# A transformer block in fp32: k, v and q by Strassen block products

## The chip, the cores and the metric

The kernel runs on one core of one Trainium2 chip. Its engines are TensorE (PE in the profile, its weight loads PEld), VectorE (DVE), ScalarE (ACT), GpSimd (POOL) and SyncE (SP), whose queue issues the DMAs here. The metric is the device time of one execution in microseconds; before the change it is 506.88 us, the median of three runs.

## The reference

From x (2048 tokens of 512 features, fp32) a layer norm without parameters gives xn. Two branches start there, and the output joins them.

```
qkv = xn @ wqkv                       # q, k, v: 32 heads of 16
pq, pk = q, k @ w_phi, head by head
phi = [softmax(p), softmax(-p)]       # over 16, so 32 per head
kv = phi_k^T v;  z = sum of phi_k over the tokens
s  = (phi_q kv / (phi_q z + 1e-6)) @ wo
g  = silu(mish(xn @ w1 + b1) @ w2)    # 512 -> 1792 -> 512
out = x + s * g
```

## The kernel before

**Exact products.** Each fp32 factor is split into a high part of type fp32r and a low part, the rest: ScalarE copies (the rounding), VectorE or GpSimd subtracts (`split`). A product of two such factors is three matmuls, low·high, high·low and high·high, accumulated in a bank of PSUM (`mm3`, or the inner loop of `product`).

**Tiles.** The tokens lie in 16 tiles of 128. Part `N` (`norm`) loads a tile of x, normalizes it, transposes it on TensorE into bank `pt`, splits it into tile `xT`, copies it raw into `xr`, and stores both to DRAM (`scr`, `raw`). Parts `K`, `V` and `Q` (`k_proj`, `v_proj`, `q_proj`) take one tile each: 4 chunks of 128 features by 3 matmuls of 128x512. The weights of k and q have w_phi folded in on TensorE (`fold`); `q_proj` loads its tile back from `scr` (tile `xq`). The softmax of k and q reads the bank and a copy of it (`kp`, `qp`), subtracts the maximum or minimum, and goes through exp on ScalarE, a sum and a reciprocal. Part `A` (`kv_acc`) adds phi_k^T v into bank `kvp`, `z` closes it, `D` (`den`) forms the denominators and transposes phi_q on VectorE into `ph`, `Ua`/`Ub` multiply with kv (`pn`), `O` (`att_out`) with wo (`pw`).

**FFN1** (parts `Fa` to `Fd`, 14 pieces n = 7 blocks of w1 by 2 halves of the tokens) uses Strassen's form already: seven products instead of eight for a 2x2 block product. Weight sums come from `P` (`prep1`) and `M` (reloaded), the x blocks and their sums from `L` (`load_g`): b11, b21, b22 from `scr`, four differences t1 to t4 from the raw tiles, then split. Accumulating sums in PSUM and additions on VectorE (`plus`) form the four output blocks. **FFN2** (`G`, closed by `E`, `final`) uses seven products too, from `R` (`prep2`), of 128x256 each; its first two of seven blocks are direct.

**Order.** Every operation is recorded first. `ORDER` lists the parts; TensorE runs their matmuls in exactly that order. For the other engines and the DMA queue a list scheduler (`simulate`) orders the operations: each has a latest time, taken from the matmul it feeds, and is started when its engine is free and its buffers fit. `copy` may go to ScalarE or VectorE, `either` to VectorE or GpSimd. `locks` names the operations that take a port shared by these two; the planned clock `port` makes the later one wait. `PEN` is added to the latest time of an operation when VectorE could leave it to another engine. Buffers: 38 slots of 4 KB per partition, 11 of 2 KB (`s2`), 2 of 16 KB (`tq`), 8 PSUM banks.

All calls are issued by line 351, so groups are told apart by tile names.

Of the kernel before, what the change touches and what calls it, by code (L numbers as in the profile page):

```python
# [28 lines left out]
PEN, HOLD, MARGIN = 2000, 300, 1000  # L29
# [8 lines left out]
wq0 wk0 N4 N2 N1 N8 wk1 wv1 wv0 N0 K1 V0 K0 K4 N5 K2 wq1 V2 N3 K5 V3 V1 K3 N9 A0 V4 V5 K8 b1 P2 N7 N6 K9 A1 A2 P3 V7  # L38
K7 K6 N12 P0 V6 N10 N11 L0 V8 K11 V9 Fa0 Fa3 K10 A3 A4 V11 V12 V10 Fb3 Fb0 Fc3 Fc0 K12 N14 Fd3 N13 P6 N15 Fd0 K14 A5
K15 V13 K13 P1 Fa1 Fa6 P4 V15 V14 Q3 Fb6 Fc6 Q2 Fb1 A7 A6 Fc1 Q0 Fd1 P5 z Q7 M2 Fa5 Fd6 D3 Fa4 Q4 Q1 Fb5 Fa2 Fc5 Fb2  # L40
Fb4 Q9 D2 Fc2 D7 Q12 Fd2 Fc4 Fd5 M4 Q5 D4 Q15 L1 Fa9 Fb9 Fd4 Fa11 Fb11 D1 Q6 Fc11 D6 M1 M6 Fc9 Fd11 Fd9 D0 Fa8 D12
Fa13 Fb13 Fc13 M0 Q10 Fb8 Fc8 Fd13 wo1 D9 D15 Fa7 D5 Fb7 Q8 Fd8 M3 Fc7 M5 Q11 Fd7 Fa10 Fa12 D8 D10 Fb12 Fb10 Fc10 Ua0
Fc12 Fd10 Fd12 Ub0 wo0 Q14 Q13 O6 D11 O1 D14 R4 O2 O7 O5 O3 D13 Ua1 O4 Ub1 O0 O11 O15 O12 O8 O13 R0 O9 R5 R1 R6 O14 G0
R2 G1 G2 R3 G3 O10 G4 G5 G6 G7 G8 G9 G10 G11 G12 G13 G14 G15 G16 G17 G18 G19 E0 G20 G21 G22 G23 G24 G25 E1 E2 G26 G27
G28 G29 G30 G31 G32 E3 G33 G34 G35 G36 G37 G38 G39 E4 G40 G41 G42 G43 G44 G45 G46 G47 E5 G48 E6 G49 G50 G51 E7
# [4 lines left out]
class Op:  # L50
    __slots__ = ("impl", "reads", "writes", "at", "idx", "succ", "ndep", "late", "new", "ready", "start", "eng", "sets", "slack", "open", "soon", "pos", "deps", "lock", "part", "half", "code")


class Program:


    def __init__(self, nc):
        self.eng = {"PE": nc.tensor, "V": nc.vector, "G": nc.gpsimd, "A": nc.scalar, "Q": nc.sync}
        self.ops, self.tag, self.cap, self.pe = [], {}, {}, []
        self.group, self.slack, self.part, self.half = None, SLACK, None, False  # L60

# [34 lines left out]

    def add(self, impl, reads, writes, sets=()):
        o = Op()
        o.code = sum(self.records(*c) for c in impl["PE"][1]) if "PE" in impl else 0
        o.impl, o.reads, o.writes, o.idx, o.sets, o.slack = impl, reads, writes, len(self.ops), sets, self.slack  # L100
        o.pos, o.part, o.half = len(self.pe), self.part, self.half
        self.half = False
        o.lock = {e for e, (_, calls) in impl.items() if any(locks(e, m, a) for m, a, k in calls)}
        if "PE" in impl:
            self.pe.append(o)
        self.ops.append(o)

    def call(self, e, m, a, k):
        aps = [v for v in list(a) + list(k.values()) if isinstance(v, bass.AP)]
        w = {aps[0].tensor.name} - {"out"}  # L110
        r = {v.tensor.name for v in aps[1:]}
# [36 lines left out]
    def links(self):  # L148
# [22 lines left out]
        for o in ops:  # L171
            o.new = []
            for n in o.reads | o.writes:
                if n in self.tag:
                    self.uses[n] = self.uses.get(n, 0) + 1
                    if n not in self.first:
                        self.first[n] = o
                        o.new.append(n)

    def simulate(self, at):  # L180
# [22 lines left out]
        dma = port = 0  # L203
# [83 lines left out]
        while left:  # L287
# [8 lines left out]
            for kind, i in todo:  # L296
# [6 lines left out]
                elif kind == 1:  # L303
                    o = ops[i]
                    left -= 1
                    for n in o.reads | o.writes:
# [15 lines left out]
            for e in ("A", "V", "G", "Q"):  # L322
                if busy[e] > now or e == "Q" and (dma > now + BACK or lanes[-LANES:][0:1] > [now] and len(lanes) >= LANES):
                    continue
                skip = []
                while ready[e]:
                    late, i = heapq.heappop(ready[e])
                    o = ops[i]
                    if o.start is not None:
                        continue  # L330
# [9 lines left out]
                for s in skip:  # L340
                    heapq.heappush(ready[e], s)
        return sorted(ops, key=lambda o: (o.start, o.idx))
# [34 lines left out]
def block_kernel(ctx: ExitStack, tc: tile.TileContext, x, wqkT, wv, phi, wo, w1, b1, w2, out):  # L377
# [98 lines left out]
    def fold(wT, name, i):  # L476
        hi = slot([P, 2, D], f"{name}h{i}", F32R)
        lo = slot([P, 2, D], f"{name}l{i}", F32R)
        for j in range(2):
            ps = bank([P, D], f"{name}f{i}{j}")  # L480
            with one():
                for g in range(KC):
                    PE.matmul(ps[:, g * P:(g + 1) * P], wT[2 * i + j][:, g, :], phit[:, g, :], start=True, stop=True)
            split(ps, hi[:, j, :], lo[:, j, :])
        return [(hi[:, j, :], lo[:, j, :]) for j in range(2)]
# [7 lines left out]
    def load_pair(src, name, i):  # L493
        t = slot([P, 2, D], f"{name}r{i}")
        Q.dma_start(t, src[2 * i * P:2 * (i + 1) * P, :].rearrange("(c p) k -> p c k", p=P))
        hi, lo = split_raw(t, f"{name}{i}")
# [3 lines left out]
    scr = [dram.tile([P, 2, KC, 4, P], F32, name=f"scr{g}") for g in range(NG)]  # L500
    raw = [dram.tile([P, KC, 4, P], F32, name=f"raw{g}") for g in range(NG)]
    xT = {}
# [6 lines left out]
    def norm(t):  # L509
# [8 lines left out]
        w = slot([P, 2, KC, P], f"xT{t}", F32R)  # L518
# [9 lines left out]
        split(pt, w[:, 0], w[:, 1])  # L528
        xT[t] = w
        xr = s2(f"xr{t}")  # L530
        copy(xr, pt.rearrange("p k n -> p (k n)"))
        Q.dma_start(raw[t // 4][:, :, t % 4, :], xr.rearrange("p (k n) -> p k n", k=KC))
        Q.dma_start(scr[t // 4][:, :, :, t % 4, :], f32(w))

    def proj(t, w, name):
        ps = bank([P, D], f"{name}{t}")
        for i in range(0, KC, 2):
            with one():
                for k in (i, i + 1):
                    mm3(ps, (xT[t][:, 0, k, :], xT[t][:, 1, k, :]), w[k], k == 0, k == KC - 1)  # L540
        return ps


    def softmax(ps, name, r):
        p = s2(f"{name}p")
        copy(p, ps)
# [22 lines left out]

    kvp = bank([P, 4, 64], "kvp")  # L570
    zacc = slot([P, 2 * D], "zacc")
    ek, eq, rq, phT, oT = {}, {}, {}, {}, {}

    def k_proj(t):
        r = sm([P, 2 * H], f"k{t}r")
        e = softmax(proj(t, w["k"], "k"), f"k{t}", r)
# [3 lines left out]
    def q_proj(t):  # L580
        xT[t] = slot([P, 2, KC, P], f"xq{t}", F32R)
        Q.dma_start(f32(xT[t]), scr[t // 4][:, :, :, t % 4, :])
        rq[t] = alloc("rq", [P, 2 * H], f"q{t}r")
        eq[t] = softmax(proj(t, w["q"], "q"), f"q{t}", rq[t])

    def v_proj(t):
        copy(vb[t % 4], proj(t, w["v"], "v"))
# [79 lines left out]
    w1_, w2_, fx, ys = {}, {}, {}, {}  # L667
# [45 lines left out]
    def load_g(q):  # L713

        def pair(k, g):
            ts = [slot([P, 2, 4 * P], f"f{'hl'[u]}{k}{g}", F32R) for u in range(2)]
            for u, t in enumerate(ts):
                Q.dma_start(f32(t.rearrange("p k n -> p (k n)")), scr[g][:, u, 2 * k:2 * k + 2].rearrange("p k t n -> p (k t n)"))
            return ts

        def whole(k, g):
            t = slot([P, 2, 4 * P], f"fr{k}{g}")
            Q.dma_start(t.rearrange("p k n -> p (k n)"), raw[g][:, 2 * k:2 * k + 2].rearrange("p k t n -> p (k t n)"))
            return t

        def sub(x, y, name):
            t = slot([P, 2, 4 * P], f"{name}{q}")
            either(t, x, y, op=ALU.subtract)
            return t

        g, h = 2 * q, 2 * q + 1
        b11, b21, b22 = pair(0, g), pair(1, g), pair(1, h)
        r11, r12, r22 = whole(0, g), whole(0, h), whole(1, h)
        t1 = sub(r12, r11, "t1")
        s1 = split_raw(t1, f"t1{q}")
        t2 = sub(r22, t1, "t2")
        s2_ = split_raw(t2, f"t2{q}")
        t3 = sub(r22, r12, "t3")
        s3 = split_raw(t3, f"t3{q}")
        t4 = sub(whole(1, g), t2, "t4")  # L740
        s4 = split_raw(t4, f"t4{q}")
        fx[q] = [b11, b21, b22, s1, s2_, s3, s4]
# [26 lines left out]
    def plus(t, ps):  # L769
        V.tensor_tensor(t, t, ps, op=ALU.add)  # L770

# [9 lines left out]
    def ffn1b(n):  # L781
        x, y = part[n][0], bank([P, D], f"fy{n}")
        product(x, n, 4, 4, False)
        part[n] += [y, held(x, f"hb{n}", 2 * (n % NB))]
        product(y, n, 3, 3, True)

    def ffn1c(n):
        x, y = part[n][:2]
        product(x, n, 5, 5, False)
        h = held(x, f"hc{n}", 2 * (n % NB) + 1)  # L790
        plus(h, y)
        put(n, h, 1, 1)

    def ffn1d(n):
        x, y, h = part.pop(n)
        product(x, n, 2, 6, False)
        put(n, held(x, f"hd{n}", 2 * (n % NB) + 1), 0, 1)
        product(y, n, 6, 2, False)
        plus(h, y)
        put(n, h, 1, 0)  # L800
# [53 lines left out]

    def final(T):
        y = lambda n: ys[T][HOME[T == NQ - 1][n][0]][:, HOME[T == NQ - 1][n][1], :]
        plus_ = lambda o, a, b: V.tensor_tensor(o, a, b, op=ALU.add)
        if T < NQ - 1:
# [13 lines left out]
            for i in range(2):  # L872
                t = 2 * T + 1 - i
# [6 lines left out]
            return  # L880
        c, u2, u3, u4 = (slot([P, D], f"yc{i}")[:, 0:2 * P] for i in range(4))
# [6 lines left out]
        for t, h, base, n in ((2 * T, 1, u5, 8), (2 * T, 0, u3, 4), (2 * T + 1, 1, u4, 3), (2 * T + 1, 0, c, 2)):  # L888
# [14 lines left out]
    w = {n: [None] * KC for n in "kqvo"}  # L903

    def weights_k(i):
        w["k"][2 * i:2 * i + 2] = fold(wkT, "wk", i)

    def weights_v(i):
        w["v"][2 * i:2 * i + 2] = load_pair(wv, "wv", i)

    def weights_q(i):
        wqT[2 * i:2 * i + 2] = load_wT(0, "wq", i)
        w["q"][2 * i:2 * i + 2] = fold(wqT, "wq", i)
# [7 lines left out]
    def sums():  # L921
# [16 lines left out]
        for i in range(4):  # L938
# [6 lines left out]
             "wk": weights_k, "wv": weights_v, "wq": weights_q, "wo": weights_o, "N": norm, "K": k_proj, "V": v_proj, "A": kv_acc, "Q": q_proj, "D": den, "Ua": num_a, "Ub": num_b,  # L945
# [39 lines left out]
```

## Time and profile before

| | |
|---|---|
| runs | 506.66, 506.88, 507.48 us |
| span of the profiled execution, first to last instruction | 505.5 us (no time of its own is listed beside it; the median is 1.4 us above) |
| mean granted TensorE clock | 0.999 |
| moved by DMA | 120.35 MB, mean 238 GB/s |
| instructions | 9803 |

Busy times are sums over an engine's instructions. A matmul's duration includes its way through the array, which the next one overlaps, so pace is read from start to start. A row names the output tile, then its inputs, with numbers left out; "idle before" is the engine's idle time just ahead of that group, and what ended it.

### The profile page before, as it was taken

Reading aid. Unit: us, or ns where it says so; the run is one execution under the profiler, and the core shown is the slowest. Engines: PE = TensorE matmul, PEld = TensorE weight load, DVE = VectorE, ACT = ScalarE, POOL = GpSimd, SP = SyncE. Lnnn points to the kernel's source line nnn. Section 1 sums busy time; section 2 is a strip of 40 time slices with the busy share of each in tenths; the row PEclk is TensorE's granted clock in tenths of the full one; section 3 lists DMA queues with packets and bytes.
Section 4 is the critical chain, followed back from the end, with each engine's and each line's share of the span. In section 5 each row is a group of like instructions: output and inputs, shape, how many; then the busy total and the mean of one; then the engine's idle time right before and its main releaser. Section 6 shows DMA issues by size and latency. Waiting matters only on the chain.

```text
span 505.5 us, 9803 instructions
## 1 busy us (share of the span) xinstructions
PE 496.5 (98%) x3594; PEld 426.6 (84%) x3594; DVE 434.1 (86%) x651; ACT 279.4 (55%) x412; POOL 378.1 (75%) x271
## 2 busy tenths in 40 slices
PE   8999999999999999999999999899999999999996
PEld 7888888888887888888888777678899999999996
DVE  5999999978879787999997899998768679978764
ACT  4865765465545332553233356587685775958611
POOL 2489999288786565686579558999789779789860
PEclk9999999999999999999999999999999999999999
DMA  8799898829987999889979762825463467665441
GB/s 307 227 336 302 294 346 278 269 105 316 294 295 251 332 319 326 291 233 318 337 240 345 255 229 78 294 89 188 146 209 118 147 204 241 236 199 171 147 146 63
DMA packets 96191, 120.35 MB, mean 238 GB/s; under 512 B 7568, under 2 KB 65040, under 8 KB 96144
## 3 DMA queue, kind: packets, MB, share of 16 engines
q1 hardware_dynamic: 96000, 119.70, 71.2%
q8 instruction: 28, 0.46, 0.4%
q14 instruction: 19, 0.16, 0.1%
q10 hardware_dynamic: 144, 0.03, 0.0%
HBM read 71.08 MB, written 48.63 MB: 237 GB/s over the span
## 4 chain that ended last, share of the span: by engine, by line
PE 89%; DVE 9%; ACT 1%; issue 0%; DMA 0%; DVEq 0%; ACTq 0%
PE y L351 28%; PE fx L351 15%; PE v L351 8%; PE fy L351 8%; PE q L351 8%; PE k L351 7%; PE pw L351 5%; PE fz L351 4%; PE pn L351 2%; PE kvp L351 2%; PE wake L351 1%; PE pt L351 1%; DVE ph L351 1%; DVE tz L351 1%; DVE ol L351 1%; DVE q13e L351 1%
## 5 line engine op out<-in xcount | busy, mean ns | idle before, releaser
L351 POOL TENSOR_TENSOR al<-r,ah 128x896 fp32r<-128x896 f32 (+1 forms) x26 | 55.0, 2123 | 11.2 <-ACT ah L351 9.7
L351 POOL TENSOR_TENSOR r<-r 128x128 f32<-128x128 f32 (+1 forms) x68 | 53.7, 808 | 4.8 <-DVE r L351 2.4
L351 ACT ACTIVATE ah<-r 128x896 fp32r<-128x896 f32 (+1 forms) x56 | 46.2, 853 | 16.5 <-POOL r L351 8.3
L351 DVE TENSOR_TENSOR al<-r,ah 128x896 fp32r<-128x896 f32 (+1 forms) x30 | 40.3, 1358 | 10.7 <-ACT ah L351 5.5
L351 ACT ACTIVATE r<-r 128x512 f32<-128x512 f32 x56 | 33.8, 624 | 19.4 <-DMA r<-hd 19.0
L351 DVE TENSOR_TENSOR r<-r 128x128 f32<-128x128 f32 (+1 forms) x52 | 38.8, 766 | 6.4 <-ACT r L351 3.5
L351 PE MATMUL k<-wkh,xT 128*128 128x512 f32 x128 | 42.2, 393 | 0.0
L351 PE MATMUL q<-wqh,xq 128*128 128x512 f32 x128 | 42.0, 393 | 0.0
L351 PE MATMUL y<-w2t,ah 128*128 128x256 f32 x224 | 40.9, 283 | 0.0
L351 PEld LDWEIGHTS y<-w2t,ah 128*128 128x128 f32 x224 | 34.9, 192 | 0.0
L351 PE MATMUL y<-w2t,al 128*128 128x256 f32 x112 | 31.7, 283 | 0.0
L351 PEld LDWEIGHTS q<-wqh,xq 128*128 128x128 f32 x128 | 24.0, 188 | 5.6 <-issue 0.7
L351 PEld LDWEIGHTS k<-wkh,xT 128*128 128x128 f32 x128 | 24.0, 188 | 5.0
L351 PE MATMUL y<-w2h,ah 128*128 128x256 f32 x96 | 27.2, 283 | 0.0
L351 PE MATMUL y<-w2l,ah 128*128 128x256 f32 x96 | 27.2, 283 | 0.0
L351 PE MATMUL y<-w2h,al 128*128 128x256 f32 x96 | 27.1, 283 | 0.0
L351 PE MATMUL k<-wkl,xT 128*128 128x512 f32 x64 | 24.9, 390 | 0.0
L351 PE MATMUL q<-wql,xq 128*128 128x512 f32 x64 | 24.9, 389 | 0.0
L351 PE MATMUL v<-wv0h,xT 128*128 128x512 f32 x64 | 23.1, 401 | 0.1
L351 PE MATMUL v<-wv1h,xT 128*128 128x512 f32 x64 | 22.3, 390 | 0.0
L351 PEld LDWEIGHTS y<-w2t,al 128*128 128x128 f32 x112 | 21.5, 192 | 0.0
L351 PE MATMUL y<-w2g,al 128*128 128x256 f32 x72 | 20.4, 283 | 0.0
(629 smaller groups left out, 1745.6 us busy)
## 6 DMA issues: line engine op xcount, KB each, us to landing
r<-hd SPq DMA_DIRECT2D x56, 256.0 KB, 3.8
scr<-xT SPq DMA_DIRECT2D x16, 512.0 KB, 5.3
xq<-scr SPq DMA_DIRECT2D x16, 512.0 KB, 5.6
w1b<-w1d SPq DMA_DIRECT2D x14, 512.0 KB, 5.7
w1b<-w1d SPq DMA_DIRECT2D x14, 384.0 KB, 4.7
x<-x SPq DMA_DIRECT2D x16, 256.0 KB, 4.7
raw<-xr SPq DMA_DIRECT2D x16, 256.0 KB, 4.6
fr<-raw SPq DMA_DIRECT2D x8, 512.0 KB, 6.4
```

Source lines behind the costliest of these rows:

```text
L351: getattr(e, m)(*a, **k)
```

## The change

Both projections become 2x2 block products over a pair of tiles (an even and an odd one).

- **x** (`norm`): tiles 2c and 2c+1 give blocks b11, b21 (even tile), b22 (odd tile) and the four differences, which VectorE forms from the two transposes and a copy of one (`xr`, now half of a tile). For the pairs 0 to 3 all seven are written into 14 slots `fh`/`fl`, which FFN1's first half, k, v and q read directly. Pairs 4 to 7 use a `tq` tile and store it to `xd`; `load_g` loads it back as 14 blocks for q and FFN1's second half. Tokens of FFN pieces are now even and odd tiles (`token`).
- **k and v** (`Ka` to `Kd`): the block matrix of weights has v and folded k as its columns, and seven products of six 128x512 matmuls per pair, in banks kx, ky, kz, replace 48 matmuls. `weights_s` forms and splits four weight sums.
- **q** (`q_proj`): the same with columns 0 to 255 and 256 to 511, in seven products of six 128x256 matmuls, all in one part. The folded weights go through DRAM (`wqd`), and `sums_q` (part `wQ`) forms the sums.
- **softmax** reads its input from SBUF, except for even k tiles.
- **FFN1**: the sixth product (y) moves from `Fd` to `Fc`, `hc` is read from y and x added.
- **Scheduler**: operations that need the port are passed over while it is taken (`PTOL`), `PEN` goes from 2000 to −1000, dependencies of x's shared slots are tracked by pieces (`region`, `names`), and `ORDER` is new: FFN1 starts among the k parts, and FFN2 parts stand among the `O` parts.

```diff
-PEN, HOLD, MARGIN = 2000, 300, 1000
+PEN, HOLD, MARGIN, PTOL = -1000, 300, 1000, 0
...
+wk0 N6 N0 wv1 N1 wk1 wv0 N2 Ka0 Ka1 N3 ws Kb0 N7 b1 Kc0 N4 Kd0 wq0 wq1 N5 Kb1 P0 Kc1 Fa0 Kd1 A0 Ka2 Kb2 Kc2 Fb0 N8 N9
...
+A4 Fc4 N15 Ka6 Kb6 A5 Ka7 Kc6 Kb7 P3 P2 P6 Kc7 Kd7 Fa6 Kd6 Fa3 Fa2 Fb3 wQ Fb6 M0 Fc3 Fc6 Fd4 A6 P1 A7 Fa1 Fb2 Fd3 Q0
+Fd6 Fc2 z D0 Fb1 Fc1 D1 L Q3 Q1 D2 Q2 Fa7 D3 Fb7 Fd1 Fd2 D4 M1 Q4 M3 Fc7 Fa10 Fd7 Fa8 D5 Fb8 D6 Fc8 M2 Fd8 D7 Fb10 Q7
...
+D14 Fc11 Fd13 O1 O4 O6 O7 R1 O0 O3 O5 R2 R0 Fd11 Fd12 G7 D15 Ua1 R4 G8 O2 Ub1 G14 G15 R5 O9 O15 O10 O8 G9 G16 R3 G17
...
+                    if e in o.lock and port > now + PTOL:
+                        held = True
+                        skip.append((late, i))
...
+        for i, a, b in ((0, x12, p0[:, 0:2]), (1, pt[:, 2:4], d[:, 0]), (2, pt[:, 2:4], x12), (3, p0[:, 2:4], d[:, 1])):
+            V.tensor_tensor(d[:, i], a, b, op=ALU.subtract)
+            if c < 4:
+                split(d[:, i], *xc[c][3 + i], either)
...
+    def kv_a(c):
+        x, z, v0 = bank([P, D], f"kx{c}"), bank([P, D], f"kz{c}"), vb[2 * c % 4]
+        kv_mm(x, c, 0, 0, True)
+        copy(v0, x)
+        kv_mm(z, c, 1, 1, True)
+        plus(v0, z)
+        kv[c] = x
+
+    def kv_b(c):
+        x, y, v1, k1 = kv[c], bank([P, D], f"ky{c}"), vb[(2 * c + 1) % 4], s2(f"k{2 * c + 1}p")
+        kv_mm(x, c, 4, 4, False)
+        copy(v1, x)
+        kv_mm(y, c, 3, 3, True)
+        copy(k1, y)
+        kv[c] = x, y, k1
+
+    def kv_c(c):
+        x, y, k1 = kv[c]
+        kv_mm(x, c, 5, 5, False)
+        plus(k1, x)
+        k_soft(2 * c + 1, k1, k1)
+        kv_mm(y, c, 6, 2, False)
+        plus(vb[(2 * c + 1) % 4], y)
+
+    def kv_d(c):
+        x, y, k1 = kv.pop(c)
+        kv_mm(x, c, 2, 6, False)
+        k0 = s2(f"k{2 * c}p")
+        copy(k0, x)
+        k_soft(2 * c, k0, x)
...
+        mm(x, 0, 0, True)
+        copy(a0, x)
+        mm(z, 1, 1, True)
+        plus(a0, z)
+        mm(x, 4, 4, False)
+        copy(a1, x)
+        mm(y, 3, 3, True)
+        copy(b1, y)
+        mm(x, 5, 5, False)
+        plus(b1, x)
+        mm(y, 6, 2, False)
+        plus(a1, y)
+        mm(x, 2, 6, False)
+        copy(b0, x)
+        for t, p in ((2 * c + 1, p1), (2 * c, p0)):
+            rq[t] = alloc("rq", [P, 2 * H], f"q{t}r")
+            eq[t] = softmax(p, p, f"q{t}", rq[t])
...
+    def weights_s():
+        s1, (v0, v1) = wraw["s"], (wraw["v", i] for i in range(2))
+        s2_, s3, s4 = (slot([P, 2, D], f"ws{i}") for i in (2, 3, 4))
+        either(s2_, s1, v0, op=ALU.subtract)
+        either(s3, v0, wraw["k"], op=ALU.subtract)
+        either(s4, v1, s2_, op=ALU.subtract)
+        for i, t in enumerate((s1, s2_, s3, s4)):
+            wkv[3 + i] = split_raw(t, f"ws{i + 1}")
```

More of the change, by code (lines that the diff above doesn't have):

```diff
@@ L50 @@
 class Op:
-    __slots__ = ("impl", "reads", "writes", "at", "idx", "succ", "ndep", "late", "new", "ready", "start", "eng", "sets", "slack", "open", "soon", "pos", "deps", "lock", "part", "half", "code")
+    __slots__ = ("impl", "reads", "writes", "at", "idx", "succ", "ndep", "late", "new", "ready", "start", "eng", "sets", "slack", "open", "soon", "pos", "deps", "lock", "part", "half", "code", "tiles")
 class Program:
@@ L172, in links @@
             o.new = []
-            for n in o.reads | o.writes:
+            for n in o.tiles:
                 if n in self.tag:
@@ L202, in simulate @@
         half = False
-        dma = port = 0
+        dma = port = told = 0
         code, fetched, cold = HEAD, 0, 0
@@ L305, in simulate @@
                     left -= 1
-                    for n in o.reads | o.writes:
+                    for n in o.tiles:
                         if n in uses:
@@ L341, in simulate @@
                     heapq.heappush(ready[e], s)
+                if held and port > told:
+                    told = port
+                    heapq.heappush(events, (port, 2, -1))
         return sorted(ops, key=lambda o: (o.start, o.idx))
@@ L474, in load_wT, with fold @@
         return ts
[L476 to L485, printed above, removed]
+    def fold(wT, name, c):
+        ps = bank([P, D], f"{name}f{c}")
+        with one():
+            for g in range(KC):
+                PE.matmul(ps[:, g * P:(g + 1) * P], wT[c][:, g, :], phit[:, g, :], start=True, stop=True)
+        return ps
     def split_raw(raw, name):
@@ L568, in scale, with plus, blocks @@
         either(e2, e2, r[:, :, None].to_broadcast([P, 2 * H, DH]), op=ALU.mult)
+    def plus(t, ps):
+        V.tensor_tensor(t, t, ps, op=ALU.add)
+    def blocks(ps, lhs, rhs, first):
+        with one():
+            for k in range(2):
+                (ah, al), (bh, bl) = lhs(k), rhs(k)
+                for i, (u, v) in enumerate(((al, bh), (ah, bl), (ah, bh))):
+                    PE.matmul(ps, u, v, start=first and k == 0 and i == 0, stop=k == 1 and i == 2, skip_group_check=True)
     kvp = bank([P, 4, 64], "kvp")
@@ L571, in block_kernel, with kv_mm, k_soft @@
     zacc = slot([P, 2 * D], "zacc")
-    ek, eq, rq, phT, oT = {}, {}, {}, {}, {}
-    def k_proj(t):
+    ek, eq, rq, phT, oT, kv = {}, {}, {}, {}, {}, {}
+    def kv_mm(ps, c, a, x, first):
+        blocks(ps, lambda k: tuple(u[:, k] for u in xc[c][x]), lambda k: tuple(t[:, k] for t in wkv[a]), first)
+    def k_soft(t, p, ps):
         r = sm([P, 2 * H], f"k{t}r")
-        e = softmax(proj(t, w["k"], "k"), f"k{t}", r)
+        e = softmax(p, ps, f"k{t}", r)
         scale(e, r)
         ek[t] = e.rearrange("p h s d -> p (h s d)")
[L580 to L584, printed above, removed]
@@ L711, in block_kernel, with load_g @@
     hd, w1d, part = {}, {}, {}
[L713 to L742, printed above, removed]
+    def load_g():
+        blocks_x(1)
+        for x in (0, 1, 4, 3, 5, 2, 6):
+            for u, t in enumerate(fx[1][x]):
+                Q.dma_start(f32(t.rearrange("p k n -> p (k n)")), xd[:, u, x].rearrange("p k j n -> p (k j n)"))
     def product(ps, n, a, x, first):
```

176 lines of the change are left out of this document (121 added, 55 removed).

## The prediction

> **What bounds the kernel now.** I read the page's busy table and its chain by engine first, then a table of windows over the stages, the chain in order of time, and last the groups of instructions that the change touches.
>
> ```profile
> PE 496.5 (98%) x3594; PEld 426.6 (84%) x3594; DVE 434.1 (86%) x651; ACT 279.4 (55%) x412; POOL 378.1 (75%) x271
> PE 89%; DVE 9%; ACT 1%; issue 0%; DMA 0%; DVEq 0%; ACTq 0%
> 0.00:16.00 16.00, 13.78 (x95) 12.94 (x95) 10.01 (x30) 8.74 (x14) 3.80 (x14) 1.00 0.80 298
> 16.00:100.00 84.00, 83.94 (x691) 69.38 (x689) 81.75 (x126) 53.08 (x79) 67.81 (x46) 1.00 0.92 293
> 100.00:300.00 200.00, 200.00 (x1294) 163.43 (x1293) 175.41 (x279) 87.45 (x124) 142.14 (x84) 1.00 0.84 283
> 295.00:323.00 28.00, 25.82 (x247) 20.10 (x258) 27.83 (x49) 17.65 (x31) 21.84 (x14) 1.00 0.57 188
> 323.00:498.00 175.00, 175.00 (x1409) 161.43 (x1378) 140.28 (x170) 112.67 (x168) 146.08 (x119) 1.00 0.53 172
> 498.00:505.50 7.50, 2.98 (x25) 2.78 (x24) 3.73 (x10) 1.13 (x3) 0.00 (x0) 0.94 0.20 70
> ```
>
> The columns of the window rows are PE, PEld, DVE, ACT, POOL. TensorE is busy for every microsecond of 100 to 300 and of 323 to 498. Its 9.0 us of idle time (505.5 − 496.5) are 2.2 at the start, 2.2 in the DVE-bound passage at 295 to 323, 4.5 at the end, and little else. The granted clock is full nearly throughout. So work taken off TensorE shortens the span, unless the new work on DVE, ACT and POOL makes it wait. DVE is the one to watch: 81.75 of 84 us in the projection stage.
>
> A busy TensorE could still be a stalled one, so the pace has to be read from start to start.
>
> ```profile
> 16.23 2.74 PE k L351 x12
> 88.17 2.72 PE k L351 x12
> 175.71 5.44 PE q L351 x24
> 399.78 0.28 PE L351 MATMUL y<-w2h,al 128*128 128x256 f32 x1
> ...
> 403.98 0.28 PE L351 MATMUL y<-w2h,ah 128*128 128x256 f32 x1
> L351 PE MATMUL k<-wkh,xT 128*128 128x512 f32 x128 | 42.2, 393 | 0.0
> L351 PE MATMUL k<-wkl,xT 128*128 128x512 f32 x64 | 24.9, 390 | 0.0
> L351 PE MATMUL q<-wqh,xq 128*128 128x512 f32 x128 | 42.0, 393 | 0.0
> L351 PE MATMUL q<-wql,xq 128*128 128x512 f32 x64 | 24.9, 389 | 0.0
> ```
>
> A 512-column matmul costs 2.72/12 = 0.2267 us of the stream. The two 256-column rows are the first and the last of 36 in one unbroken run: (403.98 − 399.78)/35 = 0.120 us. k and q have 192 matmuls each, 12 for each of 16 tiles; v has as many by the same helper.
>
> [...]
>
> **The change, part by part.**
>
> *k and v products.* For a pair of tiles, k and v together took 48 matmuls of 512 columns; seven products of six take 42. Saved: 8 pairs × 6 × 0.2267 = 10.9 us of TensorE.
>
> *q products.* A pair took 24 × 0.2267 = 5.44 us; now 42 matmuls of 256 columns, 42 × 0.120 = 5.04 us. Saved: 8 × 0.40 = 3.2 us. The weight folds, transposes, both FFN layers and the attention products keep their matmuls. Together: −14.1 us.
>
> *The bank turnaround inside a q part.* The seven q products stand next to each other in TensorE's order, and a bank is written again after only one other product, 6 × 0.120 = 0.72 us. Within that the bank must be read by ACT or DVE.
>
> ```profile
> L351 ACT ACTIVATE oh<-pn 128x256 fp32r<-128x256 f32 x32 | 10.8, 384 | 10.2 <-PE pn L351 6.1 <-DVE ol L351 4.0
> L351 DVE TENSOR_TENSOR ol<-pn,oh 128x256 fp32r<-128x256 f32 x32 | 11.9, 408 | 0.2 <-ACT oh L351 0.2
> 304.91 0.39 PE L351 MATMUL pw<-wo0h,oh 128*128 128x512 f32 x1
> 306.08 0.50 PE L351 MATMUL pw<-wo1h,ol 128*128 128x512 f32 x1 [0.78 <-DVE ol L351]
> 306.42 0.39 PE L351 MATMUL pw<-wo1l,oh 128*128 128x512 f32 x1
> L351 DVE TENSOR_TENSOR hc<-hc,fy 128x512 f32<-128x512 f32 x14 | 9.4, 674 | 1.7 <-ACT hc L351 1.6
> ```
>
> A matmul of 256 columns ends 0.28 us after its start, so 0.16 us of it lies inside the next product; with 0.38 (ACT) or 0.41 (DVE) that makes 0.54 to 0.57 of the 0.72 us, if the engine is free that instant. A started instruction ahead of it costs up to 0.67 (the hc row). A restart after a wait costs 0.34 − 0.227 = 0.11 us more, as the two pw rows show. Four turnarounds in each of 8 parts are 32: between 0 and 32 × (0.67 − 0.15 + 0.11) = 20 us. ACT is half idle, so most find it free, and the planner sees the urgency; I take the restart alone, 32 × 0.11 = +3.5 us.
>
> *The same in the k and v parts.* There the product between is 1.36 us and a 512-wide read 0.67, so 0.5 us is spare and other parts often stand between. Bounds 0 and 32 × 0.2 = 6; I take +0.5.
>
> *New work off TensorE.* Per pair of k/v three additions DVE ← PSUM, per pair of q three of half the width: 24 × 0.674 = 16.2 and 24 × 0.41 = 9.8 us of DVE. The four sums of x for each pair are DVE ← PSUM too, 8 × 4 × 0.41 = 13 us, but the second FFN preparation goes:
>
> ```profile
> L351 DVE TENSOR_TENSOR xT<-pt,xT 128x512 fp32r<-128x512 f32 x16 | 10.6, 675 | 1.7 <-ACT xT L351 1.7
> L351 POOL TENSOR_TENSOR t<-fr,t 128x1024 f32<-128x1024 f32 x4 | 10.6, 2650 | 1.2 <-DVE t L351 1.2
> L351 DVE TENSOR_TENSOR t<-fr,fr 128x1024 f32<-128x1024 f32 x2 | 3.9, 1974 | 0.0
> L351 POOL TENSOR_TENSOR wv0l<-wvr,wv0h 128x1024 fp32r<-128x1024 f32 x1 | 2.4, 2409 | 2.7 <-ACT wv0h L351 2.7
> L351 DVE TENSOR_TENSOR t20l<-t,t20h 128x1024 fp32r<-128x1024 f32 x1 | 1.2, 1225 | 0.1
> L351 ACT ACTIVATE wv0h<-wvr 128x1024 fp32r<-128x1024 f32 x1 | 1.1, 1099 | 0.0
> ```
>
> The x work comes out nearly even on DVE and falls on POOL. The sums of the weights are new: for k/v three subtractions and four splits of 128x1024, for q four half-sized sums and the splits, at 1.2 us on DVE or 2.4 on POOL. With 7 × 1.2 = 8.4 for k/v, DVE gains about 16.2 + 9.8 + 8.4 = 34 us at most. I cost it at nothing: DVE is idle for 505.5 − 434.1 = 71 us, FFN1 of the first half now starts among the k/v parts and gives TensorE long products with little DVE work, and part of DVE's time is waiting (below). If that cover is gone, it is the last rival.
>
> *Passing over port operations, and the smaller penalty for DVE.* These alter only the orders on DVE and POOL.
>
> ```profile
> L351 DVE TENSOR_TENSOR r<-r 128x128 f32<-128x128 f32 x36 | 26.4, 746 | 1.1 <-POOL r L351 1.0
> L351 POOL TENSOR_TENSOR r<-r 128x128 f32<-128x128 f32 x44 | 30.0, 697 | 3.5 <-DVE r L351 2.4 <-PE y L351 0.6
> ```
>
> DVE takes 746 ns for 128 columns from SBUF, and 408 for 256 from PSUM: the first was waiting, POOL being at work on SBUF. [...] No gain of its own: the stages where these rows stand have TensorE full. Bounds ±2.2 us through the passage at 295 to 323; taken with that passage.
>
> *The start.* TensorE's first k product was at 16.23. Now the first two parts need only v's raw weights and even tiles, but the next needs the fold of k, two sums and their splits on engines that also serve six norms. The chain is about 1.4 + 1.2 + 1.1 + 1.2 = 4.9 us of DVE and ACT at the rows above, against 5.4 us of TensorE work in Ka0 and Ka1. Bounds −1 and +6 (seven 1024-wide operations, shared by POOL at 2.4 and DVE at 1.2 us, take 5.6); I take +2.
>
> *DMA.* Stores and loads of x's splits and raw tiles fall away and the sums come back once.
>
> ```profile
> scr<-xT SPq DMA_DIRECT2D x16, 512.0 KB, 5.3
> xq<-scr SPq DMA_DIRECT2D x16, 512.0 KB, 5.6
> fr<-raw SPq DMA_DIRECT2D x8, 512.0 KB, 6.4
> SPq L351 <- ACT xr L351: 15.8, 7, 7.9
> SPq L351 <- DVE xT L351: 12.8, 4, 8.0
> ```
>
> q no longer waits for xq, and with the 32 stores of x the two waits of SP's queue shown here (15.8 and 12.8 us, hidden now) shrink to those of eight larger stores and two of wqd; what stands behind a waiting store there, tile loads and later the stores of FFN1, moves up. But the loads of the second half's 14 blocks (7 MB, about 24 us at the 293 GB/s of the second window) need the slots that the first half holds until Q2, two parts before Fb7. While they wait, SP's queue holds back the FFN1 stores behind them, for which nobody waits before FFN2. Bounds 0 and 6.4, one landing; I take +1.5. The extra wqd round trip lies behind the k stage: 0.
>
> *FFN1's regrouping* has the same products, evictions and additions: 0. *The passage at 295 to 323* has FFN2 parts (G7, G8, G14 to G18) among the output projections now, which can fill the 2.2 us: bounds −2.2 and +3, I take −1.5.
>
> Sum on the profiled span: 505.5 − 14.1 + 3.5 + 0.5 + 2.0 + 1.5 − 1.5 = 497.4 us. The median of the runs is 506.88, 1.4 us above the span; adding that, 498.8 us.
>
> **The rivals.**
>
> *Clean gain.* The planner covers turnarounds, start and slots, and only −14.1 and −1.5 remain: 489.9 + 1.4 = 491.3 us. For it: 375 us in the trace without a gap on TensorE. Against it: 0.15 us of slack for 32 turnarounds.
>
> *The gain is spent where it is earned.* Turnarounds cost twice my figure, start and slots half of their upper bounds: 505.5 − 14.1 + 7 + 0.5 + 3 + 3.2 − 1.5 = 503.6, 505.0 in the runs, and 502 to 507 around it. For it: TensorE's order is fixed, so no other part can slip into a wait.
>
> *VectorE, with the port, becomes the bound of the projections (slower).* Place: the first 100 us and the q parts. Price: of the 34 us of new DVE work, what isn't covered lies on the path. It decides once 14.1 of the 34 (four tenths) is uncovered; at six tenths, 505.5 − 14.1 + 20.6 = 512.0, 513.4 in the runs. For it: 81.75 of 84 us busy and the port waits. Against it: FFN1 spread over the stage, and POOL relieved of the x sums.
>
> *The change does not do what it says*, the matmuls being fewer but no shorter in sum: excluded by 0.120 and 0.227.
>
> **How the numbers follow.** My forecast (495 to 502) has a chance of 0.46, the clean gain 0.20, the spent gain 0.20, the DVE bound 0.14. The likeliest gives 498.8. The range 491 to 507 reaches to the clean gain and takes in the spent gain; it leaves out the DVE bound and a sliver below. 0.2% is 1 us, about what a measurement of this kernel tells from no change: faster (below 505.9) 0.46 + 0.20 + three quarters of the spent gain = 0.81; within 0.2% 0.05; slower 0.14, the DVE bound.
>
> **What would show it.** Fewer projection matmuls: k and v in rows kx, ky, kz at 0.227, q at 0.120 from start to start. Gaps before every second q product would show the turnarounds; gaps in the first 30 us, before the products of ws, the start; gaps before Fb7, the slots. The PE share should stay at 97 to 98%. The prediction is wrong if DVE's share of the chain grows well beyond 9% with gaps on TensorE in the first 100 us, or if TensorE is as full as now at a span near 490.

## The result, and the profile after

The changed kernel takes 511.5 us, the median of four runs (510.6 to 512.0); the kernel before took 506.8 us beside it (506.1 to 507.5). The ratio is 1.0089, interval 1.0075 to 1.0103: slower by 0.9%, where 498.8 us were forecast with a range of 491 to 507. The profiled execution has a span of 508.9 us, against 505.5.

First the busy table and the chain by engine of the changed kernel, from its page:

```profile
PE 489.9 (96%) x3690; PEld 424.9 (83%) x3690; DVE 455.6 (90%) x830; ACT 282.1 (55%) x433; POOL 280.7 (55%) x204
PE 81%; DVE 13%; DMA 2%; ACT 1%; issue 1%; POOL 1%; SPq 0%; DVEq 0%; ACTq 0%
```

DVE's share of the chain went from 9% to 13% and TensorE's from 89% to 81%. TensorE is busy for 6.6 us less in a span 3.4 us longer. The table of windows of the same kernel (columns as before: PE, PEld, DVE, ACT, POOL, granted clock, DMA share, GB/s) says where:

```profile
0.00:25.00 25.00, 18.28 (x91) 15.38 (x92) 20.09 (x52) 14.13 (x23) 15.39 (x20) 0.88 0.71 243
50.00:100.00 50.00, 49.19 (x462) 39.61 (x461) 48.45 (x94) 27.68 (x41) 43.96 (x31) 1.00 0.57 190
100.00:150.00 50.00, 49.16 (x338) 40.01 (x337) 48.90 (x79) 26.49 (x38) 38.86 (x27) 1.00 0.71 243
250.00:300.00 50.00, 48.70 (x484) 40.45 (x483) 47.00 (x84) 24.83 (x44) 36.16 (x23) 1.00 0.58 195
300.00:350.00 50.00, 46.89 (x433) 37.22 (x432) 48.01 (x83) 29.68 (x54) 34.76 (x23) 0.97 0.53 175
```

TensorE has gaps in the first 25 us, with a clock of 0.88, and small ones in stages where it was full before; DVE is busy for 94 to 98% of the later ones.

For the sums I count a matmul's gap as its interval from start to start, less the usual interval of its shape (the median: 0.227 us at 512 columns, 0.120 at 256, 0.111 at 128, 0.016 and 0.007 for the small matmuls of `pn` and `kvp`), over all matmuls of a trace but the first dummies (`wake`). "Matmul stream" is the sum of these usual intervals. A slower pace at a lower clock counts as a gap, too. The rows below the second belong to the experiments; each is one profiled execution, in us, and that of the third row took 499.5 us, 1.7 less than the median beside it.

| kernel | runs, median | matmul stream | gaps to 50 us | 50 to 300 | 300 to 350 | later | all gaps |
|---|---|---|---|---|---|---|---|
| before | 506.8 | 479.3 | 3.3 | 6.9 | 4.6 | 0.1 | 14.9 |
| changed | 511.5 | 465.1 | 11.7 | 14.0 | 6.2 | 1.0 | 32.9 |
| changed, wait at the port | 501.2 | 465.1 | 10.7 | 9.9 | 1.6 | 0.1 | 22.3 |
| the same, from 250 us on | 506.6 | 465.1 | 11.7 | 14.1 | 2.0 | 0.1 | 27.9 |
| the same, up to 250 us | 504.3 | 465.1 | 10.9 | 9.7 | 6.3 | 0.1 | 27.0 |
| changed, no additions to v | 507.6 | 465.1 | 10.8 | 13.2 | 4.9 | 0.1 | 29.0 |
| wait, no additions to v | 499.9 | 465.1 | 9.8 | 9.7 | 2.0 | 0.1 | 21.6 |
| wait, k's banks emptied early | 499.6 | 465.1 | 9.8 | 9.8 | 2.1 | 0.1 | 21.8 |
| wait, no sums of weights | 498.8 | 465.1 | 8.0 | 10.9 | 1.9 | 0.1 | 20.8 |

The products did what they should: 14.2 us less of matmuls. The gaps grew by 18.0 us.

One gap, traced back in the timeline of the changed kernel (start, duration, engine, then the operation; its wait in brackets):

```profile
81.20 2.40 POOL L372 TENSOR_TENSOR zacc<-zacc,k4e 128x1024 f32<-128x1024 f32 x1
81.26 2.88 DVE L372 TENSOR_TENSOR k7e<-k7m,k7p 128x512 f32<-128x512 f32 x1
...
89.52 0.62 DVE L372 TENSOR_TENSOR k6e<-k6m,kx 128x512 f32<-128x512 f32 x1
...
90.20 0.50 PE L372 MATMUL fz<-fh,w1al 128*128 128x512 f32 x1 [0.79 <-DVE k6e L372]
```

TensorE waits for k6e, the last reader of a bank. DVE is late there by 2.2 us lost nine microseconds earlier: k7e takes 0.68 us when zacc does not start ahead of it (the timeline of the first experiment, below, has it), and 2.88 here, since GpSimd had begun an addition to zacc 0.06 us before. For zacc nobody waits but the next addition to it, until part z. The rows show DVE behind the whole of that operation: k7e, whose two inputs lie in SBUF, ends at 84.14, 0.54 us after zacc (83.60), so 0.06 us of lead cost 2.20 us. GpSimd's being busy is not enough: the 16 additions to v, one input of which is a bank of PSUM, all overlap operations of GpSimd in this trace, eight of them from start to end, and take 0.63 to 0.68 us. The trace of the kernel before has it the other way round, too: GpSimd's w21l, started at 320.81 while DVE's q13e ran (to 321.93), takes 3.35 us, and w2l, of the same shape, 2.38 at 328.54. This is what "the port" stands for here.

The largest single gap, from the same timeline:

```profile
320.84 1.29 POOL L372 TENSOR_TENSOR al<-r,ah 128x512 fp32r<-128x512 f32 x1
320.88 1.33 DVE L372 TENSOR_TENSOR tz<-tz,q15r 128x64 f32<-128x64 f32 x1
...
327.16 1.51 POOL L372 TENSOR_TENSOR al<-r,ah 128x512 fp32r<-128x512 f32 x1 [4.33 <-ACT ah L372]
327.47 1.48 DVE L372 TENSOR_TENSOR w2r<-w2r 128x256 f32<-128x256 f32 x1
...
328.88 1.29 DVE L372 STREAM_TRANSPOSE ph<-q15e 128x512 f32<-128x512 f32 x2
...
329.72 3.67 PE L372 MATMUL pn<-ph,kvw 32*32 32x256 f32 x103 [3.11 <-DVE ph L372]
```

Twice in 7 us an operation of DVE starts 0.04 and 0.31 us behind one of GpSimd; tz lasts 1.33 us where 0.21 would do, and w2r 1.48 for 0.41 (as in the first experiment's trace); they end 0.08 and 0.28 us after the operation of GpSimd. The transposes that Ua1 needs come after them, and TensorE stands for 3.1 us.

A third place shows an operation on as few as 32 columns that loses the same way, and ends 0.04 us after GpSimd's (two views of the changed kernel, DVE and GpSimd first, then TensorE):

```profile
248.78 3.46 POOL L372 TENSOR_TENSOR ez<-q8e,zb 128x1024 f32<-128x1024 f32 x1 [1.59 <-DVE q6r L372]
249.90 2.38 DVE L372 SCALAR_TENSOR_TENSOR den<-tz 128x32 f32<-128x32 f32 x1
...
258.75 0.39 PE L372 MATMUL qx<-wq1h,fl 128*128 128x256 f32 x1 [1.30 <-DVE q11p L372]
```

In the first experiment's trace this den takes 0.18 us, ez comes after it, and the wait of 1.30 us is gone.

### The profile page after: what moved, and what is told of

It reads as the page before. It is cut to its first block, busy times and chain, and to the rows that moved or that the text cites. A ratio compares the mean times of both kernels' runs of the same rounds, so it can differ in the third digit from the quotient of the medians.

```text
span 508.9 us, 10014 instructions
## 1 busy us (share of the span) xinstructions
PE 489.9 (96%) x3690; PEld 424.9 (83%) x3690; DVE 455.6 (90%) x830; ACT 282.1 (55%) x433; POOL 280.7 (55%) x204
## 4 chain that ended last, share of the span: by engine, by line
PE 81%; DVE 13%; DMA 2%; ACT 1%; issue 1%; POOL 1%; SPq 0%; DVEq 0%; ACTq 0%
PE y L372 25%; PE fx L372 14%; PE kx L372 8%; PE fy L372 7%; PE pw L372 5%; PE qx L372 4%; PE fz L372 4%; PE ky L372 3%; PE pn L372 2%; PE qy L372 2%; DVE tz L372 2%; PE kz L372 2%; PE kvp L372 1%; DVE ph L372 1%; DMA r<-hd 1%
## 5 line engine op out<-in xcount | busy, mean ns | idle before, releaser
L372 POOL TENSOR_TENSOR r<-r 128x128 f32<-128x128 f32 (+1 forms) x18 | 10.7, 600 | 92.4 <-DVE r L372 58.6
L372 DVE TENSOR_TENSOR al<-r,ah 128x896 fp32r<-128x896 f32 (+1 forms) x45 | 44.9, 1017 | 9.3 <-ACT ah L372 5.1
L372 PE MATMUL fx<-fh,w1b 128*128 128x512 f32 x112 | 38.6, 392 | 0.0
L372 POOL TENSOR_TENSOR al<-r,ah 128x896 fp32r<-128x896 f32 (+1 forms) x11 | 20.6, 1875 | 21.4 <-ACT ah L372 21.4
L372 PEld LDWEIGHTS fx<-fh,w1b 128*128 128x128 f32 x112 | 21.0, 188 | 5.1 <-DVE ha L372 0.4
L372 PE MATMUL fx<-fl,w1b 128*128 128x512 f32 x56 | 21.9, 391 | 0.0
L372 POOL TENSOR_TENSOR w1sl<-w1s,w1sh 128x1024 fp32r<-128x1024 f32 x7 | 16.8, 2412 | 8.7 <-ACT w1sh L372 8.7
L372 PE MATMUL y<-w2m,ah 128*128 128x256 f32 x72 | 20.4, 283 | 0.0
L372 PE MATMUL y<-w2g,ah 128*128 128x256 f32 x72 | 20.4, 283 | 0.0
L372 PE MATMUL fy<-fh,w1b 128*128 128x512 f32 x56 | 19.6, 390 | 0.0
## 6 DMA issues: line engine op xcount, KB each, us to landing
w1b<-w1d SPq DMA_DIRECT2D x14, 512.0 KB, 4.6
w1a<-w SPq DMA_DIRECT2D x7, 512.0 KB, 4.9
w1d<-w1sh SPq DMA_DIRECT2D x7, 512.0 KB, 2.7
```

The source lines that it names most:

```text
L372: getattr(e, m)(*a, **k)
```

## The experiments

**Theory and rivals.** *Order theory:* the new rule passes over port operations while the port is taken, so the plan gives it to DVE's short operation at an exact moment. On the chip nothing enforces this: GpSimd's next instruction starts as soon as its own data are there, takes the port first, and DVE, with no time to spare, hands the delay to TensorE. *Load theory:* DVE simply has too much work (455.6 us). *Start:* its gaps (+8.4 us in the first 50 us) need not come from either.

**1. The plan's order enforced one way.** An operation of GpSimd that uses the port also waits for the last such operation of VectorE that the plan has ahead of it:

```diff
+                i = getattr(e, m)(*a, **k)
+                if locks(o.eng, m, a):
+                    if o.eng == "V":
+                        port = i.ins.name
+                    elif port is not None:
+                        tc.add_manual_dep(i.ins, port, ...)   # GpSimd waits
```

> Every GpSimd operation that needs the shared port also waits for the last VectorE operation on the port that was planned ahead of it; each engine's own order and all the work are those of the changed kernel. Order theory (the new scheduler rule lets VectorE go first at the port in the plan, while on the chip GpSimd, already waiting, takes it and VectorE's short operation stands behind a 2.4 us one; VectorE's order is full, so the delay reaches TensorE): the waits of TensorE after the start shrink, 496 to 503 us. Load theory (VectorE simply has too much work, 455.6 us of 508.9, whoever goes first): 511.5 within 1.5 us, or some us more for the added waits.

Measured: 501.2 us (499.2 to 502.1), ratio to before 0.9879 (0.9860 to 0.9898): 10 us regained, and a kernel faster than before. Its timeline at the two places above:

```profile
79.03 0.68 DVE L372 TENSOR_TENSOR k7e<-k7m,k7p 128x512 f32<-128x512 f32 x1
...
82.53 2.40 POOL L372 TENSOR_TENSOR zacc<-zacc,k4e 128x1024 f32<-128x1024 f32 x1 [3.46 <-DVE w1al L372]
...
319.70 0.41 DVE L372 TENSOR_TENSOR w2r<-w2r 128x256 f32<-128x256 f32 x1
...
320.24 1.30 POOL L372 TENSOR_TENSOR al<-r,ah 128x512 fp32r<-128x512 f32 x1 [2.28 <-DVE w2r L372]
...
320.88 2.75 PE L372 MATMUL pn<-ph,kvw 32*32 32x256 f32 x128
```

zacc waits for DVE, and k7e and w2r are back at 0.68 and 0.41 us. That zacc now waits until w1al, an operation of DVE behind k7e, also shows that the plan had k7e ahead of zacc. Ua1 (last row) starts without a wait. GpSimd is idle for 3.5 and 2.3 us, and no wait of TensorE follows from it in this trace.

**2. Both ways.** VectorE waits for GpSimd's port operations ahead of it in the plan, too (the same edit, with the engine kept beside the name).

> As the run before, and VectorE's operations on the port wait for GpSimd's that were planned ahead of them: the whole planned order at the port. Order theory: like the run before or 1 to 2 us better, 495 to 502 us. Load theory: 511.5 or more, since VectorE, the full engine, gets more waits: 512 to 518 us.

Measured: 503.0 us, ratio 0.9935 (0.9914 to 0.9956). A gain again, but less than with one, where the order theory had as much or more: a small miss. That VectorE now waits for the engine that has time is my reading, not tested further. So what is shown is that GpSimd must not take VectorE's turn; that the whole planned order would be best is not. All further experiments use the first form.

**3. The old rule on the changed kernel.**

```diff
-PEN, HOLD, MARGIN, PTOL = -1000, 300, 1000, 0
+PEN, HOLD, MARGIN, PTOL = 2000, 300, 1000, 1 << 30
```

> The Strassen projections and the new ORDER, with the old scheduler rule: port operations are not passed over, and the penalty for VectorE is 2000 again. GpSimd then gets more of the shared work and VectorE less. Load theory: VectorE is relieved, 500 to 511 us. Order theory: the old rule counts the wait at the port as the chip does, so plan and chip agree, but ORDER was drawn up for the other rule: slower than 515 us, by tens of us if long waits stand before TensorE's next part.

Measured: 580.1 us, ratio 1.1438 (1.1421 to 1.1454). Its page:

```profile
PE 511.2 (89%) x3690; PEld 437.4 (76%) x3690; DVE 488.3 (85%) x749; ACT 282.2 (49%) x436; POOL 394.2 (68%) x282
PE 56%; DVE 18%; POOL 12%; issue 5%; ACT 4%; DMA 3%; SPq 0%; POOLq 0%; DVEq 0%; ACTq 0%
```

GpSimd has 113 us more and the chain runs through it for 12%. This order of the parts stands or falls with the rule: what the prediction took for a detail holds 69 us here. The penalty and the passing over go back together in this run; what each holds was not separated.

**4. The new rule alone, on the kernel before** (PEN, PTOL and the passing over; products and parts' order as they were).

> The kernel before (no Strassen projections, old ORDER) with the new scheduler rule alone: port operations passed over, penalty -1000. Order theory: the plan's order at the port is not the chip's, and work moves to VectorE: 510 to 520 us, with new waits of TensorE behind VectorE. Load theory: VectorE was at 434 of 505 us and has no Strassen additions to carry: 504 to 509 us.

Measured: 517.1 us, ratio 1.0203 (1.0189 to 1.0216). The rule by itself costs 10 us without any Strassen product in k, v or q.

**5. The wait on the kernel before.**

> The kernel before, with the same wait as in the first experiment and nothing else: an operation of GpSimd that needs the port waits for the last such operation of VectorE that the plan has ahead of it. Order theory: the plan before let the later of two engines wait for the port, just as the chip does, and its end of TensorE agrees with the trace within about 2 us, so there is no order to restore: 505 to 508 us, no change. If the wait helps for a reason of its own (fewer collisions at the port, whatever the plan), the kernel before gains too, several us: 498 to 503.

Measured: 507.9 us, ratio 1.0029 (1.0017 to 1.0041). No gain, a small loss. The wait is no improvement by itself; it mends the new plan.

**6. Less load on DVE, same order.** At issue, 16 additions are skipped:

```diff
+            if o.eng == "V" and o.impl["V"][1][0][0] == "tensor_tensor" and any(n[0] == "v" and n[1].isdigit() for n in o.writes):
+                continue
```

> The changed kernel in its own order on every engine, but without the 16 additions of the second product to v (v<-v,kz and v<-v,ky, 16 x 0.672 = 10.8 us of VectorE, all in the stage where VectorE has no idle time; v stays incomplete). They read PSUM and so need no port. Load theory (VectorE's sum of work is the bound there): most of the 10.8 us goes, 501 to 504 us. Order theory (the delays come from a few places where VectorE waits for the port, and between them it catches up): hardly anything goes, 509 to 512.

Measured: 507.6 us, ratio 1.0020 (1.0008 to 1.0033). About 4 of the 10.8 us come back: both numbers missed. The load seems to have a share. It is smaller than 4, for the 3.1 us ahead of Ua1 stayed as they were, and 1.3 us of the gain lie in the 128 matmuls behind them, which took 2.75 us in this profile and 4.08 in the changed kernel's.

**7. The new rule and the wait on the kernel before.**

> The kernel before, with the new scheduler rule and penalty (517.1 us in the fourth experiment) and with the wait of the first experiment. Order theory: the rule's planned order is restored and a good part of the 10 us comes back, 511 to 514; the rest is that the parts' order was not chosen for this rule. It tells also how much of the 501.2 us of the first experiment is owed to Strassen's products and the parts' new order rather than to the rule. If the wait does nothing here: 516 to 518.

Measured: 515.4 us, ratio 1.0170 (1.0157 to 1.0183). Only 1.7 us come back, less than expected. On this kernel most of the rule's 10 us are therefore not turns that GpSimd took; that they lie in the plan, whose order of parts was not chosen for the rule, is my reading and was not tested. With the same rule and wait the changed kernel is 14 us ahead (501.2 against 515.4), about as much as its matmuls are shorter, though the orders of parts differ too.

**8 and 10. The start: k's banks emptied early.** With the wait, Ka1 stands for 2.9 us before a bank that the fold of k holds until wkl has read it. Four operations move ahead:

```diff
+        for e, n, b in (("A", "wkh1", "ws3h"), ("V", "wkl1", "mv3")):
+            mine = [o for o in seq if o.eng == e and any(w.startswith(n) for w in o.writes)]
...
+            seq[i:i] = mine        # ahead of the first o that writes b
```

> The first experiment's kernel (wait added to the changed one, 501.2 us), with the two copies and two subtractions that empty the banks of k's second fold (wkh, wkl) moved ahead in the orders of ScalarE and VectorE, before ws3h and before the norm of tile 3. If the 3.06 us wait of Ka1 for one of these banks, and the seven matmuls at half clock behind it (1.4 us), are a price of their own: 496.5 to 498.5. If the start is bound by the sums of the weights (ws2l and ws1l are formed by GpSimd at 2.4 us each, and Kb0 needs them), the wait moves from Ka1 to Kb0 and only 0 to 1.5 us go: 499.5 to 501.5.

Measured: 499.6 us, ratio 0.9858 (0.9844 to 0.9872). The gaps are read from the second run of the same kernel.

> The eighth experiment's kernel again (wait, and the banks of k's second fold emptied earlier), for a profile of its start: the eighth's profiled execution ran its matmuls at a third of the pace and its gaps cannot be read. 499.5 us; Ka1 without its 3 us wait for a bank, and a new wait of 1.5 to 2.5 us ahead of Kb0, on ws2l or on tile 3's transposes, if the sums of the weights bound the start.

Measured: 499.6 us, ratio 0.9856 (0.9841 to 0.9871), the fastest kernel that computes the whole. The waits of the second run, in its timeline:

```profile
19.45 0.47 PE L378 MATMUL kx<-wv0h,fl 128*128 128x512 f32 x1 [1.07 <-DVE wkl L378]
...
24.14 0.63 PE L378 MATMUL pt<-ident,x 128*128 128x128 f32 x4 [1.68 <-DVE v L378]
...
27.05 0.50 PE L378 MATMUL ky<-ws1h,fl 128*128 128x512 f32 x1 [0.90 <-DVE xs L378]
```

The 2.9 us became 1.1 (first row), 1.7 ahead of tile 3's transposes and 0.9 ahead of ws1's product. The gaps to 50 us fall only from 10.7 to 9.8: the bank alone was not the bound.

**9. Less load, with the wait.** The edit of the sixth on the first.

> The first experiment's kernel (changed kernel with the wait, 501.2 us) without the 16 additions to v that the sixth experiment left out (10.8 us of VectorE; v stays incomplete). In the plain changed kernel leaving them out gave 4 us. If VectorE's load is a cause of its own, as large here: 497 to 498. If the load only matters because it keeps VectorE from catching up after the port was taken in the wrong order: 500 to 502, nothing gained.

Measured: 499.9 us, ratio 0.9867 (0.9853 to 0.9880), against 0.9879 (0.9860 to 0.9898): no difference that can be told (21.6 us of gaps in all against 22.3). With the turns kept, 10.8 us of DVE's work are hidden. The load theory falls as a cause of its own; that the load decides whether a lost turn can be made up fits the sixth and this run.

**11 and 12. Where the wrong turns cost.** The wait for one part of the plan alone:

```diff
-                    elif port is not None:
+                    elif port is not None and o.start >= 250000:   # e12: < 250000
```

> The changed kernel with the first experiment's wait only for operations that the plan starts at 250 us or later. If the loss comes from single wrong turns at the port close to where TensorE waits (the 3.3 us before Ua1 at 329.7 above all): most of the 10 us goes, 501 to 503. If VectorE carries a lag from turns lost long before and pays it in that passage: little goes, 506 to 510.

> The other half: the wait only for operations that the plan starts before 250 us. Single wrong turns: only the small gaps up to 275 us go (about 4 us by the gaps of the two traces), 506 to 508. Carried lag: most goes, 500 to 504. The two halves need not add up to the whole, if a late wrong turn costs nothing to a VectorE that comes without a lag.

Measured: 506.6 us (ratio 0.9993, 0.9984 to 1.0002) and 504.3 us (0.9952, 0.9939 to 0.9964): 4.9 and 7.2 us, together a little more than the whole. By these times the carried lag did better: 506.6 lies in its 506 to 510, and 504.3 just above its 500 to 504. But the gaps decide, and against it. From 250 us on (eleven), in its timeline:

```profile
81.49 2.93 DVE L372 TENSOR_TENSOR k7e<-k7m,k7p 128x512 f32<-128x512 f32 x1
...
90.47 0.50 PE L372 MATMUL fz<-fh,w1al 128*128 128x512 f32 x1 [0.79 <-DVE k6e L372]
...
325.69 0.41 DVE L372 TENSOR_TENSOR w2r<-w2r 128x256 f32<-128x256 f32 x1
...
326.87 2.75 PE L372 MATMUL pn<-ph,kvw 32*32 32x256 f32 x128
```

Up to 250 us (twelve):

```profile
79.16 0.68 DVE L372 TENSOR_TENSOR k7e<-k7m,k7p 128x512 f32<-128x512 f32 x1
...
321.88 1.48 DVE L372 TENSOR_TENSOR w2r<-w2r 128x256 f32<-128x256 f32 x1
...
324.13 3.94 PE L372 MATMUL pn<-ph,kvw 32*32 32x256 f32 x128 [3.12 <-DVE ph L372]
```

Each half removes its own gaps and leaves the others (14.1 us from 50 to 300 and 2.0 from 300 to 350, against 9.7 and 6.3, in the table). Ua1 starts without a wait in eleven, where the early turns are lost, and waits its 3.12 us in twelve, where they are kept: single wrong turns, paid some microseconds later, and no lag carried over 200 us. My numbers for it were off in part because the early gaps, 5.1 us to 300, sum to more than the 4 that I had read from the traces.

**13. The start without the sums of the weights.** Products 3 to 6 use split weights that exist already, the sums are not formed, and the plan is made anew (the loop alone is shown):

```diff
-        for i, t in enumerate((s1, s2_, s3, s4)):
-            wkv[3 + i] = split_raw(t, f"ws{i + 1}")
+        for i, j in enumerate((2, 0, 0, 1)):
+            wkv[3 + i] = wkv[j]
```

> The first experiment's kernel (changed kernel with the wait, 501.2 us) without the four sums of the weights of k and v: products 3 to 6 use the split weights of k, v0, v0 and v1 in their place (k and v are wrong then), planned anew. It leaves out about 1.4 + 3 x 1.2 us of sums and four splits, two or three of them at 2.4 us on GpSimd. Gaps on TensorE in the first 50 us are 10.8 us with the sums and 3.4 us in the kernel before. If the sums of the weights bound the start: 4 to 6 us of gaps, 495 to 498 in all. If the start is bound by the two tiles of x that a part needs now, with their norms, splits and differences on VectorE, and by the first weights: 8.5 to 11 us of gaps remain there, 499 to 502 in all.

Measured: 498.8 us, ratio 0.9843 (0.9827 to 0.9859). The gaps of the first 50 us go from 10.7 to 8.0, 2.7 of the 7.4 that they have above the kernel before. Its waits of TensorE from 8 to 50 us, summed (total, times, longest):

```profile
PE kx L372 <- POOL wv0l L372: 1.7, 1, 1.7
PE kz L372 <- POOL wv1l L372: 1.5, 1, 1.5
PE kx L372 <- DVE v L372: 0.8, 1, 0.8
```

The first two are the low parts of v's weights, which GpSimd forms in 2.4 us; the prediction did not count them. The second wait is new with this plan: in the first experiment's kernel VectorE forms wv1l, in 1.21 us, and TensorE does not wait for it. And 1.4 of the 2.7 us are a stretch at half pace in the first experiment's profile that this one does not have. So the sums have a part in the start; how large a part stays open.

## Why the prediction was wrong, by its steps

**The step that failed** is "Passing over port operations, and the smaller penalty for DVE", with the new work of DVE beside it: costed at nothing, with bounds of ±2.2 us, because "these alter only the orders on DVE and POOL" and TensorE was full where the waiting rows stood. Keeping GpSimd from taking VectorE's turns regained 10.3 us (511.5 to 501.2); that is the price of this step. The reason given was wrong in kind. TensorE was full under an order made with the later of the two engines waiting at the port, as the traces have it for both (3.35 us of w21l, 2.88 us of k7e; the fifth experiment found nothing to mend there); the new order relies on turns that were not kept, such as that of k7e ahead of zacc. This is shown for the changed kernel; on the kernel before, the same rule cost 10 us of which the wait gave back 1.7. Mean durations hid it. The group that the prediction showed waiting, at 746 ns, is this one in the changed kernel (groups of DVE, shapes kept apart):

```profile
L372 DVE TENSOR_TENSOR r<-r 128x128 f32<-128x128 f32 x68 | 23.6, 368 | 1.6 <-POOL r L372 0.9
```

Most of it no longer waits: 63 of the 68 rows last 0.28 to 0.30 us, five last 0.67 to 2.21. What costs time now are single rows such as k7e at 2.88 us, in places that TensorE stands behind. Of the 10.6 us of gaps that the wait removes (32.9 to 22.3), 6.0 are four waits of TensorE beyond 50 us that are then gone: 0.8 at 90.20, 0.8 at 142.69, 1.3 at 258.75 and 3.1 at 329.72. Among the rest are 1.3 of slower pace behind the last of them, 1.0 at the start and a wait of 0.7 at 480.42.

**The start**, +2.0 (bounds −1 to +6): +8.4 in the changed kernel and +7.4 with the wait, beyond the bound. In the changed kernel TensorE waits 1.66 us for wv0l and 3.53 us ahead of Ka1, and behind each of these waits its matmuls go at half pace for a while, 1.7 and 1.4 us more than at the usual pace; with the restarts these four make 8.7 of the 11.7 us. In its timeline:

```profile
15.01 0.50 PE L372 MATMUL kx<-wv0l,fh 128*128 128x512 f32 x1 [1.66 <-POOL wv0l L372]
...
16.89 0.63 PE L372 MATMUL kz<-wv1h,fl 128*128 128x512 f32 x1
17.32 0.63 PE L372 MATMUL kz<-wv1l,fh 128*128 128x512 f32 x1
...
22.92 0.77 PE L372 MATMUL kx<-wv0h,fl 128*128 128x512 f32 x1 [3.53 <-DVE nb L372]
```

Emptying the bank ahead of Ka1 earlier (eight and ten) or leaving out the sums (thirteen) took 0.9 and 2.7 us and brought other waits. What keeps these engines late (the sums, or pairs of tiles with their norms and differences, on a DVE with hardly an idle microsecond) was not separated. The window from 25 to 50 us of the first experiment's kernel:

```profile
25.00:50.00 25.00, 23.93 (x189) 20.12 (x188) 24.14 (x51) 18.27 (x35) 22.57 (x23) 1.00 0.37 137
```

DVE, the third number, is busy for 24.14 of 25 us there.

**Right:** the products, −14.1 forecast, −14.2 by the table (479.3 to 465.1), where the counts are as given and the paces are measured; the q part runs at 0.120:

```profile
239.50 0.28 PE L372 MATMUL qx<-wqh,fl 128*128 128x256 f32 x1
...
240.82 0.28 PE L372 MATMUL qz<-wq1h,fh 128*128 128x256 f32 x1
240.93 0.35 PE L372 MATMUL qx<-wqs0h,fl 128*128 128x256 f32 x1
241.13 0.27 PE L372 MATMUL qx<-wqs0l,fh 128*128 128x256 f32 x1
```

Eleven intervals take 1.32 us, and the restart on bank qx takes 0.20 instead of 0.12. The turnarounds: +3.5 for q and +0.5 for k and v, 1.4 and 1.3 with the wait (k and v from 50 us on), so 2.7 for 4.0; the q parts of the changed kernel have 2.8, of which 1.46 is one wrong turn at 258.8.

**Too dear or too cheap, smaller:** the slots before Fb7, +1.5, cost nothing that the trace shows. The passage at 295 to 323, −1.5, gave −3.0 (4.6 to 1.6 in the column of 300 to 350) with the order kept, and +1.6 without.

Together, with the order kept: −14.2 + 7.4 + 3.0 (50 to 300 us, 2.7 of it turnarounds) − 3.0 = −6.8 against a forecast of −8.1, a near hit that owes something to luck, since the start was 5.4 too cheap and three others (turnarounds, slots, passage) 1.2 to 1.5 too dear; the wrong turns add 10.6 of gaps. The rival that came closest is the one of DVE and the port, 513.4 with a chance of 0.14, and the sign that the prediction had named for being wrong came: DVE's share of the chain at 13%, with gaps in the first 100 us. Its price was near, in part by luck, and half its mechanism: it spoke of uncovered load, and the same load is covered once the turns are kept (nine).

## What to carry to other kernels

When a scheduler plans a shared resource, ask what on the chip enforces the plan: here an order across two engines that no semaphore held went to the one that started first, and a lead of 0.06 us cost 2.20 us. A short operation of the busy engine that stands behind a long one of the idle engine is the sign to look for, in single rows and not in means. One wait on the engine that has time to spare gave back 10.3 us here; on a plan that had counted the port's waits it gave nothing, and on a third plan 1.7 us.

## What was not expected of the hardware

After TensorE had stood for 1.66 us at the start, the 512-column matmuls of the changed kernel followed each other at 0.43 us instead of 0.227 (16.89 and 17.32 above) from 15.61 to 19.00, at a granted clock of 0.51 (15.6 to 19.0), and again from 23.48 to 25.62 behind the 3.53 us, at 0.50 (23.5 to 25.6); behind the 3.1 us ahead of Ua1 the clock is 0.50 from 329.7 to 333.0, and 0.97 over the window from 300 to 350. So these gaps cost more than their length. Others did not: behind the same first wait, 1.69 us there, the first experiment's kernel kept its pace and went at 0.43 later, behind its 2.90 us ahead of Ka1; the sixth ran at full pace behind 3.13 us ahead of Ua1; and the thirteenth had a clock of 1.00 over the first 25 us with waits of 1.7 and 1.5 in them. What decides it is not shown. And the wait that gained 10.3 us on GpSimd alone gained 8.5 when VectorE had it too.
